# A dynamic convolution and squared-ReLU feed-forward kernel: the four-slot convolution from the sixth block on instead of the ninth

## The chip, the cores and the metric

The kernel runs on one core of one Trainium2 chip. The metric is the time of one execution in device microseconds (us). Five engines work side by side, each through its own list of instructions in order: PE (the matrix engine), DVE and ACT (vector and scalar engine), POOL and SP. In this kernel SP and POOL mainly issue transfers (DMAs); SP also issues the stores of the result. Tiles live in SBUF, a memory of 128 partitions; PE writes to PSUM, from which ACT and DVE copy.

## The reference, cut to what matters

```python
# dynamic convolution: x (8, 4096, 192), weight_gen (8, 4096, 8 heads, 7 taps)
w = softmax(weight_gen, over the 7 taps)
x_pad = six zero rows ahead of each sequence
out[b, s, h, g] = sum over k of w[b, s, h, k] * x_pad[b, s + k, 24 * h + g]
# feed-forward on the 32768 rows of out: 192 -> 2048 -> 192
h = maximum(out @ moe_w_in, 0)
return h * h @ moe_w_out
```

Each of the 8 heads owns 24 of the 192 columns and has its own seven weights at each position.

## The kernel before, in words

The 32768 positions are 64 sub-blocks of 512. They are worked in 33 blocks, counted from 0 here: the first two blocks hold one sub-block each, blocks 2 to 32 hold two. A block's work has four parts.

*Weights and bands.* ACT takes the exponential of the raw weights (line 238), DVE sums, inverts and multiplies (245, 252, 260) into `v_first` or `v_big`. For the first batch and the first half of the second these rows go by DMA from SBUF to the tiles `wr`, alternately on SP and POOL (`move_rows`, line 351); later they go through DRAM (`vd`). DVE multiplies `wr` with a mask into the band tiles `bd` (`st_bands`, line 391).

*The convolution, C.* PE multiplies the loaded `x` rows (`xt`, loaded on POOL, lines 311 to 321) with the bands into PSUM, and ACT or DVE copy the result as float16 to `y`, which has the channels on the partitions and 512 positions along the row, for two halves at once (partitions 0 to 63 and 64 to 127). There are two forms:

- The old form (`st_conv`, line 519) puts the 192 channels into three slots of 64. A tile of 32 partitions then holds parts of two heads, and each needs its own matmul with its own band: 120 matmuls of 8 to 32 columns for a block. ACT makes both copies (line 530).
- The four-slot form (`st_conv_spread`, line 485) gives each head a tile of 32 partitions with 24 used rows. Heads 0 to 5 take slots 0 to 2, heads 6 and 7 a fourth slot: 80 matmuls. ACT copies slots 2 and 3, DVE slots 0 and 1 (line 495). Then four DMAs on SP (line 499) move heads 6 and 7 in pieces of 8 rows from the fourth slot into the free rows of the other three, so that the matmuls that follow read three full slots in both forms.

Because the rows stand in another order, blocks with the four-slot form use `w_p`, a copy of `w_in` with its rows permuted in the same way. `load_w_spread` fills it with 16 DMAs from DRAM on POOL (lines 156 and 163), and `cross_w_spread` with two more that exchange the halves (line 169).

*The units, u.* Each block has 16 units (`st_unit`). PE makes 128 of the 2048 hidden channels from `y` and `w_i` or `w_p` (line 564) in a PSUM tile `h`, of which there are three, shared with C; ACT applies the ReLU (line 578), DVE squares it into `g` (line 582), two units at a time but for the last two.

*The second matmul, M.* Eight steps a block, two for each quarter of the positions, multiply the `g` of the block before with `w_o` (line 613). After the second of a quarter ACT copies one PSUM bank (line 627) and DVE adds the other (line 629); only then may the next quarter write there, as there is only one such pair of banks.

The order of all this is written out by hand, in strings of steps, and every engine keeps it. For blocks 0 to 3 the strings are spelled out in `plans`. From block 4 on two strings are used, and a table (`fill`) adds the softmax pieces (E, S), band steps (B) and weight loads (L) at certain units:

```python
steady = "MuMuuu" * 3 + "MuuuMCu"
steady_spread = "MuMuuu" * 2 + "MuCMuuu" + "MuMuuu"
```

A C in block j makes the convolution of block j + 1; it is followed by the x loads for block j + 2 on POOL. The four-slot form is used for blocks from `FIRST_SPREAD = 8` on, and the same name decides from which block on `steady_spread` is used and where the band steps stand. `load_w_spread` is issued after the C of block 5, `cross_w_spread` after that of block 6.

Of the kernel before, what the change touches and what calls it, by code (L numbers as in the profile page):

```python
# [9 lines left out]
def kernel(  # L10
# [34 lines left out]
    HK = H * KK  # L45
    G = D // H
    SPREAD = H - 2
    FIRST_SPREAD = 8
    HP = H // 2

    P = 128
# [87 lines left out]
    def cross_w_in(q):  # L139
        for r0, r1 in ((0, RT), (RT, 0)):  # L140
            nc.sync.dma_start(out=w_i[r0 : r0 + RT, q, 1], in_=w_i[r1 : r1 + RT, q, 0])
# [322 lines left out]
    def st_conv_spread(j):  # L464

        s0, n = BLOCKS[j]
        y = p_y.tile([P, NK + 1, TB], f16, name="y")
        y_t[j] = y
        for ks in ((NK, NK - 1), (0, 1)):
            yp = ps_h.tile([P, 2, TB], f32, name="yp", tag="h")  # L470
            k0 = min(ks)
            for k in ks:
                for i in range(NT):
                    a, b = bounds[i], bounds[i + 1]
                    for half in (0, 1):
                        s = s0 + half
                        hi = a + (STEP if tile_start(s, i) == starts[i] else b - a)
                        bd = bd_t[s][:, H * a : H * hi].rearrange(
                            "p (g c e) -> p g e c", g=HP, e=2
                        )  # L480
                        for e in (0, 1):
                            head = 2 * k + e
                            p0 = RT * half + 32 * e
                            c0 = min(G * head, D - 32)
                            nc.tensor.matmul(  # L485
                                out=yp[p0 : p0 + 32, k - k0, a:b],
                                lhsT=x_t[s][:, i, c0 : c0 + 32],
                                rhs=bd[:, head // 2, e, 0 : b - a],
                                start=True,
                                stop=True,  # L490
                                skip_group_check=True,
                                tile_position=(0, p0),
                            )
            copy = nc.vector.tensor_copy if k0 == 0 else nc.scalar.copy
            copy(out=y[:, k0 : k0 + 2], in_=yp)  # L495
        for p0 in range(0, P, 32):
            head = SPREAD + p0 // 32 % 2
            r0 = p0 + G * head - min(G * head, D - 32)
            nc.sync.dma_start(out=y[p0 + G : p0 + 32, 0:NK], in_=y[r0 : r0 + G, NK])

    def st_conv(j):

        if j >= FIRST_SPREAD:
            return st_conv_spread(j)
        if j < NFIRST:
            return st_conv_first(j)
        y = p_y.tile([P, NK, TB], f16, name="y")
        y_t[j] = y
        yps = [ps_h.tile([P, 2 * TB], f32, name="yp", tag="h") for _ in range(2)]
        for later, s, i, q, half, a, b, base in conv_pieces(j):  # L510
            lo = bounds[i]
            hi = lo + (STEP if tile_start(s, i) == starts[i] else bounds[i + 1] - lo)
            _, ha, hb, pre = quads[q]
            m, h = (32, hb) if later else (pre, ha)
            bd = bd_t[s][:, H * lo : H * hi].rearrange("p (g c e) -> p g e c", g=HP, e=2)
            p0 = RT * half + 32 * (q % 2)
            k = q // 2
            col = TB * (k % 2) - base
            nc.tensor.matmul(  # L519
                out=yps[k // 2][p0 : p0 + m, col + a : col + b],  # L520
                lhsT=x_t[s][:, i, 32 * q : 32 * q + m],
                rhs=bd[:, h // 2, h % 2, a - lo : b - lo],
                start=True,
                stop=True,
                skip_group_check=True,
                tile_position=(0, p0),
            )
        for n, yp in enumerate(yps):
            k0, k1 = 2 * n, min(2 * n + 2, NK)
            nc.scalar.copy(  # L530
                out=y[:, k0:k1],
                in_=yp[:, 0 : (k1 - k0) * TB].rearrange("p (k c) -> p k c", c=TB),
            )
# [20 lines left out]
    def st_unit(j, u):  # L554

        w = w_p if j >= FIRST_SPREAD else w_i
        h = ps_h.tile([P, 2, TB], f32, name="h", tag="h")
        if j < NFIRST:
            first_unit(u, h, y_t[j])
        else:  # L560
            for slot in range(NK):
                for half, r0 in enumerate((0, RT)):
                    k = slot ^ half if slot < 2 else slot
                    nc.tensor.matmul(  # L564
                        out=h[:, half],
                        lhsT=w_in_chunk(w, u, slot, half),
                        rhs=y_t[j][r0 : r0 + RT, k],
                        start=(slot == 0), stop=(slot == NK - 1),
                        skip_group_check=True,
                        tile_position=(r0, 0),  # L570
                    )
        e = u % 2
        if e == 0:
            t1_t[j] = p_t1.tile([P, 2, 2, TB], f16, name="t1")
            gp_t[j] = p_g.tile([P, 2, 2, TB], f16, name="g")
        t1, g = t1_t[j], gp_t[j]
        g_t[(j, u)] = g[:, e]
        nc.scalar.activation(out=t1[:, e], in_=h, func=ActF.Relu)  # L578
        n = 2 if j < NFIRST or u < NF - 2 else 1
        if e + 1 >= n:  # L580
            a = e + 1 - n
            nc.vector.tensor_tensor(  # L582
                out=g[:, a : e + 1], in0=t1[:, a : e + 1], in1=t1[:, a : e + 1], op=AluOp.mult
            )
# [63 lines left out]
    with nc.allow_low_precision("fp16 matmul pipeline"), tc.manual_schedule():  # L648
# [71 lines left out]

        steady = "MuMuuu" * 3 + "MuuuMCu"
        steady_spread = "MuMuuu" * 2 + "MuCMuuu" + "MuMuuu"
        plans = {
            0: "B1 u u u u E1 C S1 u u M u u",
# [9 lines left out]
        def at(j, u, kind, *args):  # L736
            fill.setdefault((j, u), []).append((kind, *args))
# [36 lines left out]
        for j in range(len(plans), NBLK - 1):  # L774
            a = BLOCKS[j + 1][0]
            small = [p for p in parts if p.fb <= j + 1][-1].r == FIRST
            us = {4: (7, 9), 6: (7, 9)}.get(j, (5, 9) if small else (1, 5))
            if j + 1 >= FIRST_SPREAD:
                us = (1, 5)
            for n, u in enumerate(us):  # L780
                at(j, u, "B", a + n)
        for j in range(len(plans), NBLK):
            plan, u = [], 0
            for step in steady_spread if j + 1 >= FIRST_SPREAD else steady:
                if step == "u":
                    plan += [f"{kind}{n}" for kind, n in fill.get((j, u), ())]
                    u += 1
                plan.append(step)
            plans[j] = " ".join(plan)
# [3 lines left out]
        def load_rows(j):  # L793

            s = [p for p in parts if p.fb <= j][-1]
            if s.r == FIRST:
                return
            if s in stored:
                for n in range(BLOCKS[j][0], sum(BLOCKS[j])):
                    wr_load(n)  # L800
            else:
                waiting.append((s, j))
# [40 lines left out]
        for j in range(NBLK):  # L843
            if j + 2 < NBLK:
                load_rows(j + 2)
            if j == 1:
                for q in range(WQ):
                    cross_w_in(q)
            u = 0
            for step in plans[j].split():  # L850
                kind, n = step[0], int(step[1:] or 0)
                if kind == "u":
                    st_unit(j, u)
                    u += 1
                elif kind == "M":
                    next(mm2)
                elif kind == "C" and j + 1 < NBLK:
                    st_conv(j + 1)
                    if j == 0:
                        x_load(3)  # L860
                    elif j + 2 < NBLK:
                        for k in range(BLOCKS[j + 2][0], sum(BLOCKS[j + 2])):
                            x_load(k)
                    if j == 5:
                        load_w_spread()
                    elif j == 6:
                        cross_w_spread()
                elif kind == "E":
                    parts[n].exp(*next(parts[n].exps))
                elif kind == "S":  # L870
                    soft(parts[n])
                elif kind == "B":
                    st_bands(n)
                elif kind == "L":
                    parts[n].load(nc.sync)


        j = NBLK - 1
# [44 lines left out]
```

The softmax here doesn't subtract the row's maximum and nothing guards it: scores larger than these inputs give would overflow.

## Time and profile before

| | us |
|---|---|
| median of three runs | 733.32 (732.42 to 733.91) |
| the profiled execution | 733.26 |
| its span, first to last instruction | 731.5 |
| PE busy | 724.6 |
| DVE busy | 626.1 |
| ACT busy | 612.8 |
| POOL busy | 100.0 |

The profile is that of one execution. The span is shorter than the execution's time by what lies around the instructions. A busy time is the union of an engine's instructions. The chain that ended last gives each engine and line its share of the path that set the end. A timeline line shows the start within the span, the length, the engine, the line of the code, the operation and how many instructions were merged; in brackets stands the idle time before it and what ended it. The letters dq or q behind an engine name its queue: SPq lines are the issues of transfers, not the transfers.

Line numbers are those of the kernel before.

### The profile page before, as it was taken

How to read it: one execution, taken by the hardware profiler on the slowest of the kernel's cores; microseconds unless marked ns; L12 is line 12 of the kernel's file. 1: busy time of each engine (PE TensorE's matmuls, PEld its weight loads, DVE VectorE, ACT ScalarE, POOL GpSimd, SP SyncE). 2: the span in 40 equal slices, each digit the busy share in tenths (PEclk: the TensorE clock that was granted, in tenths of full speed). 3: DMA queues.
4: the chain of work that ended last, by engine and by line, in shares of the span. 5: the costliest groups of instructions: out<-in, count | busy, mean ns of one | idle time of the engine just before them, and what ended most of it. 6: DMA issues, size and time to landing. Idle time of an engine off the chain costs nothing.

```text
span 731.5 us, 30985 instructions
## 1 busy us (share of the span) xinstructions
PE 724.6 (99%) x14053; PEld 529.2 (72%) x14053; DVE 626.1 (86%) x834; ACT 612.8 (84%) x731; POOL 100.0 (14%) x145
## 2 busy tenths in 40 slices
PE   8999999999999999999999999999999999999998
PEld 4557788777777777777777777777777777777777
DVE  6898998998898988888988888988889988778753
ACT  5999888888888888888888888888888888888883
POOL 8232222321001100011000010010000110001000
PEclk9999999999999999999999999999999999999999
DMA  9555444784445452455433554334544315444012
GB/s 204 115 105 115 82 76 109 146 150 118 98 66 136 87 94 57 86 117 114 72 69 68 124 116 87 56 73 120 103 87 86 57 50 120 66 87 78 30 45 68
DMA packets 125984, 68.30 MB, mean 93 GB/s; under 512 B 85321, under 2 KB 122140, under 8 KB 125340
## 3 DMA queue, kind: packets, MB, share of 16 engines
q0 software_dynamic: 46192, 19.43, 22.5%
q1 hardware_dynamic: 79516, 46.79, 22.5%
q8 instruction: 110, 1.80, 1.0%
q14 instruction: 22, 0.18, 0.1%
q10 hardware_dynamic: 144, 0.10, 0.0%
HBM read 50.18 MB, written 28.70 MB: 108 GB/s over the span
## 4 chain that ended last, share of the span: by engine, by line
PE 92%; DVE 2%; issue 1%; DMA 0%; ACT 0%; DVEq 0%
PE o L613 45%; PE h L564 42%; PE yp L485 4%; PE yp L519 1%; DVE bd L391 1%; DVE g L582 1%; DMA wr<-v_first 0%; ACT t L578 0%; DVE v_first L260 0%; DVE rcp L252 0%; DVE ssum L245 0%; PE h L549 0%; DVE o_sb L629 0%; ACT o_sb L627 0%; DVEq L391 0%
## 5 line engine op out<-in xcount | busy, mean ns | idle before, releaser
L578 ACT ACTIVATE t<-h 128x1024 f16<-128x1024 f32 x512 | 496.6, 1026 | 60.3 <-PE h L564 58.9
L613 PEld LDWEIGHTS <-g 64*128 64x128 f16 (+1 forms) x8032 | 344.6, 94 | 54.9 <-issue 2.3
L613 PE MATMUL o<-w_o,g 64*128 64x192 f16 (+1 forms) x8032 | 380.4, 243 | 0.2 <-DVE o_sb L629 0.2
L582 DVE TENSOR_TENSOR g<-t 128x2048 f16<-128x2048 f16 (+1 forms) x287 | 307.4, 1105 | 28.3 <-ACT t L578 28.1
L564 PE MATMUL h<-y,w_p 64*128 64x512 f16 x2400 | 291.7, 376 | 0.0
L564 PEld LDWEIGHTS <-w_p 64*128 64x128 f16 x2400 | 113.9, 94 | 94.7
L391 DVE TENSOR_TENSOR bd<-wr,mask 128x4160 f16<-128x4160 f16 (+3 forms) x89 | 149.4, 1703 | 2.1 <-DMA wr<-v_first 1.2
L629 DVE TENSOR_TENSOR o_sb<-o,o_sb 128x384 f32<-128x384 f32 x123 | 68.4, 556 | 62.2 <-ACT o_sb L627 61.1
L321 POOL DMA_DIRECT2D xt<-in_x_dram x63 | 53.0, 844 | 415.2 <-PE yp L485 362.4
L627 ACT COPY o_sb<-o 128x384 f32<-128x384 f32 x129 | 61.7, 478 | 45.5 <-PE o L613 45.0
L564 PE MATMUL h<-y,w_i 64*128 64x512 f16 x576 | 70.8, 376 | 0.2 <-ACT y L530 0.2
L564 PEld LDWEIGHTS <-w_i 64*128 64x128 f16 x576 | 31.2, 94 | 21.4 <-issue 1.4
L485 PEld LDWEIGHTS <-xt 128*32 128x32 f16 x2000 | 24.4, 95 | 10.6 <-issue 10.6
L260 DVE TENSOR_TENSOR v_big<-ex,rcp 128x112 f16<-128x112 f32 (+5 forms) x180 | 29.9, 237 | 1.9 <-DMA vd<-v_big 0.9
L495 DVE CAST y<-yp 128x1024 f16<-128x1024 f32 x25 | 30.5, 1218 | 0.0
L485 PE MATMUL yp<-bd,xt 128*32 128x104 f16 (+1 forms) x2000 | 28.3, 210 | 0.0
L238 ACT ACTIVATE ex<-wg 128x560 f32<-128x560 f32 (+4 forms) x38 | 25.9, 683 | 2.0 <-DMA wg<-in_weight_gen_dram 2.0
L245 DVE TENSOR_REDUCE ssum<-ex 128x80 f32<-128x560 f32 (+4 forms) x38 | 25.3, 666 | 1.5 <-ACT ex L238 1.5
L495 ACT CAST y<-yp 128x1024 f16<-128x1024 f32 x25 | 25.2, 1006 | 0.0
L252 DVE RECIPROCAL rcp<-ssum 128x80 f32<-128x80 f32 (+4 forms) x38 | 22.8, 600 | 1.3
L311 POOL DMA_DIRECT2D xt<-in_x_dram x7 | 3.9, 555 | 123.8 <-PE yp L485 109.4
L351 POOL DMA_DIRECT2D wr<-v_first x24 | 12.9, 562 | 22.8 <-ACT t L578 12.2
(40 smaller groups left out, 117.2 us busy)
## 6 DMA issues: line engine op xcount, KB each, us to landing
out_dram<-o_sb SPq DMA_DIRECT2D x63, 384.0 KB
xt<-in_x_dram POOLq DMA_DIRECT2D x42, 240.0 KB, 4.8
wg<-in_weight_gen_dram SPq DMA_DIRECT2D x4, 1064.0 KB
xt<-in_x_dram POOLq DMA_DIRECT2D x21, 192.0 KB, 4.7
wr<-vd SPq DMA_DIRECT2D x38, 80.0 KB
vd<-v_big SPq DMA_DIRECT2D x5, 512.0 KB
y<-y SPq DMA_DIRECT2D x100, 24.0 KB
wg<-in_weight_gen_dram SPq DMA_DIRECT2D x3, 616.0 KB
```

The costliest lines, as they stand in the source:

```text
L238: nc.scalar.activation(out=self.ex[:, lo:hi].rearrange("p r g k e -> p (r g) k e"), in_=self.wg[:, lo:hi].rearrange("p r (g e) k -> p (r g ...
L260: eng.tensor_tensor(out=bass.AP(tensor=v.tensor, offset=v.offset + lo * H * SL + lo % SL * 2 + g * SL * 2, ap=[list(v.ap[0]), [H * SL + 2, ...
L321: eng.dma_start(out=dst[:, first:last], in_=ap)
L391: nc.vector.tensor_tensor(out=bd_t[j][:, H * lo : H * (lo + len(tiles) * n)].rearrange("p (g m c) -> p g m c", g=shape[1], c=2 * SL), in0= ...
L485: nc.tensor.matmul(out=yp[p0 : p0 + 32, k - k0, a:b], lhsT=x_t[s][:, i, c0 : c0 + 32], rhs=bd[:, head // 2, e, 0 : b - a], start=True, sto ...
L495: copy(out=y[:, k0 : k0 + 2], in_=yp)
L564: nc.tensor.matmul(out=h[:, half], lhsT=w_in_chunk(w, u, slot, half), rhs=y_t[j][r0 : r0 + RT, k], start=(slot == 0), stop=(slot == NK - 1 ...
L578: nc.scalar.activation(out=t1[:, e], in_=h, func=ActF.Relu)
L582: nc.vector.tensor_tensor(out=g[:, a : e + 1], in0=t1[:, a : e + 1], in1=t1[:, a : e + 1], op=AluOp.mult)
L613: nc.tensor.matmul(out=oo[:, cc * Dm : (cc + 1) * Dm], lhsT=g[r0 : r0 + n, cc * P : (cc + 1) * P], rhs=w_o[r0 : r0 + n, fc, :], start=(fc ...
L627: nc.scalar.copy(out=o_sb, in_=o[0][:, c])
L629: nc.vector.tensor_tensor(out=o_sb, in0=o[1][:, c], in1=o_sb, op=AluOp.add)
```

## The change

The four-slot form is used from block 5 on instead of block 8, so in three more blocks (5, 6 and 7). What else hung on the name `FIRST_SPREAD`, the choice of the string and the band steps, stays at 8 under a new name, `EARLY_CONV`. In `steady`, which orders blocks 4 to 6, C moves ahead of the last M. The 16 loads of `w_p` are issued after the C of block 1, behind the x loads there, and the two exchanges after the C of block 2.

```diff
-    FIRST_SPREAD = 8
+    FIRST_SPREAD = 5
+    EARLY_CONV = 8
...
-        steady = "MuMuuu" * 3 + "MuuuMCu"
+        steady = "MuMuuu" * 3 + "MuuuCMu"
...
-            if j + 1 >= FIRST_SPREAD:
+            if j + 1 >= EARLY_CONV:
                 us = (1, 5)
...
-            for step in steady_spread if j + 1 >= FIRST_SPREAD else steady:
+            for step in steady_spread if j + 1 >= EARLY_CONV else steady:
...
-                    if j == 5:
+                    if j == 1:
                         load_w_spread()
-                    elif j == 6:
+                    elif j == 2:
                         cross_w_spread()
```

## The prediction

> **What bounds the kernel now.** I read the page first (busy shares, the chain that ended last), then the PE timeline around two block boundaries, then ACT, DVE, SP and POOL over the same microseconds, and last the trace's DMA records.
>
> The page, its busy shares and the chain that ended last:
>
> ```profile
> span 731.5 us, 30985 instructions
> ...
> PE 724.6 (99%) x14053; PEld 529.2 (72%) x14053; DVE 626.1 (86%) x834; ACT 612.8 (84%) x731; POOL 100.0 (14%) x145
> ...
> PE o L613 45%; PE h L564 42%; PE yp L485 4%; PE yp L519 1%; DVE bd L391 1%; DVE g L582 1%; DMA wr<-v_first 0%; ACT t L578 0%; DVE v_first L260 0%; DVE rcp L252 0%; DVE ssum L245 0%; PE h L549 0%; DVE o_sb L629 0%; ACT o_sb L627 0%; DVEq L391 0%
> ```
>
> PE sets the end and is never idle for long: whatever PE is spared comes off the time, and whatever PE waits for is added. So I cost everything as PE time.
>
> PE's timeline where block 4 goes over into block 5 (columns: start, length, engine, line, operation):
>
> ```profile
> 95.43 1.48 PE L613 MATMUL o<-w_o,g 64*128 64x192 f16 x32
> 96.84 1.60 PE L519 MATMUL yp<-bd,xt 128*32 128x104 f16 x120
> 98.38 0.82 PE L564 MATMUL h<-y,w_i 64*128 64x512 f16 x6
> 99.03 1.66 PE L613 MATMUL o<-w_o,g 64*128 64x192 f16 x32
> 100.45 0.89 PE L564 MATMUL h<-y,w_i 64*128 64x512 f16 x6
> ```
>
> The order is M (a second-matmul step), C (120 matmuls), u15, M, and at 100.45 u0 of block 5, the first reader of the new y. From 95.43, which I call T, to u0 it is 5.02 us. At the next two boundaries T is 118.09 and 140.71 and u0 comes at 123.07 and 145.62 (4.98, 4.91).
>
> PE where block 7 makes the first four-slot conv:
>
> ```profile
> 156.07 0.81 PE L564 MATMUL h<-y,w_i 64*128 64x512 f16 x6
> 156.82 1.13 PE L485 MATMUL yp<-bd,xt 128*32 128x104 f16 x80
> 157.88 1.49 PE L613 MATMUL o<-w_o,g 64*128 64x192 f16 x32
> ```
>
> DVE and SP after that conv:
>
> ```profile
> 158.53 1.22 DVE L495 CAST y<-yp 128x1024 f16<-128x1024 f32 x1
> ```
>
> ```profile
> 159.82 3.01 SPq L499 DMA_DIRECT2D y<-y  x4
> ```
>
> The four-slot y isn't complete with the copies: four 24 KB moves on SP follow the DVE copy. In the DMA records I took, for each of the 25 such convs, when the last of the four landed after the DVE copy ended: 4.9 to 6.5 us, median 5.4, and 4.4 for the last one, which has no x loads beside it. Here they landed at 165.92; the first reader is at 167.70. Nobody waits, because seven units and three M lie between conv and reader.
>
> ACT and DVE at the end of block 4:
>
> ```profile
> 94.34 2.85 ACT L578 ACTIVATE t<-h 128x1024 f16<-128x1024 f32 x3
> ```
>
> ```profile
> 94.22 4.09 DVE L582 TENSOR_TENSOR g<-t 128x2048 f16<-128x2048 f16 x4
> 98.23 0.55 DVE L629 TENSOR_TENSOR o_sb<-o,o_sb 128x384 f32<-128x384 f32 x1
> ```
>
> The relu of the third unit ends at 97.19 (T+1.76), the square of it on DVE at 98.31 (T+2.88; T+2.78 and T+2.77 at the other two).
>
> [...] the undisturbed last case lands 4.4 us after the copy, of which the fourth issue begins 2.1 to 2.2 us in. [...] the wr loads issued on POOL at 59.11 landed 3.7 us later, just behind the x loads issued at 55.48 (6.3 to 6.9 us to landing). [...]
>
> **The change, part by part.**
>
> Conv matmuls: 3 blocks x (120 - 80). Old boundary: M at 95.43 and u15 at 98.38 are 2.95 apart, less 1.32 for a plain M is 1.63. New kind: 156.07 to 157.88 is 1.81, less 0.65 for the unit is 1.16. Saved 0.47 a block, 1.4 in all. The same from block periods: 22.54 between old convs (74.30, 96.84) against 22.08 between new ones (156.82, 178.90).
>
> Copies: ACT loses the 594 ns half copy of each block and DVE gains the 1.22 us one. The order of ACT's and DVE's instructions in the changed kernel puts both y copies ahead of the o copy and the o sum of the M that now follows C.
>
> The y moves, the main term. In blocks 4, 5 and 6 the order becomes u u u C M u15, and the next block opens with M, u0. Counting from T for block 4: conv 95.52 to about 96.7, M to 98.0, u15 to 98.65. The DVE copy is queued behind the squares, so it runs 98.31 to 99.53; the o sum behind it ends at 100.0. The opening M needs that bank, so it runs 100.0 to 101.4 instead of from 98.65. But u0 needs the four moves: 99.53 + 5.4 = 104.95 against 100.45 before, a loss of 4.5. The other two: 120.87 + 1.22 + 5.4 = 127.5 against 123.07 (4.4) and 143.48 + 1.22 + 5.4 = 150.1 against 145.62 (4.5). Sum +13.4; these are u0-to-u0 differences, so the 1.4 saved and the wait of the opening M are inside. The squares can't come earlier, since ACT's relu of the third unit bounds them. Bounds: landing 4.9 gives 11.9, landing 6.2 gives 15.8. On SP only an output store stands behind the moves, with nobody waiting for it. Behind the waiting u0 stands all of PE; ACT and DVE catch up meanwhile, so nothing later is late, but a bound PE doesn't win the time back.
>
> The loads of w_p. They leave POOL's queue at 123 and 148, where nobody waited (gain nothing), and enter at 43.3, behind the x loads of conv 2. POOL before:
>
> ```profile
> 42.43 0.84 POOL L321 DMA_DIRECT2D xt<-in_x_dram  x1
> ...
> 59.11 2.72 POOL L351 DMA_DIRECT2D wr<-v_first  x5 [2.87 <-DVE v_first L260]
> ```
>
> The 16 loads took 12.3 us at 123.23 to 135.56, with 3.1 of waiting for landings eight DMAs back; so from 43.3 to about 55.5. The x loads of block 4 (before: 54.08) go to about 55.6 to 57.8. The two crossing moves wait until the loads have landed (median 5.7 us), about 60.3, and hold POOL till then; behind them stand the wr loads of sub-blocks 6 and 7, and then the x loads issued after conv 4, not due before 96.84. So the wr loads are issued at 61.7 instead of 59.11. In the ring they stand behind 768 KB of crossing, which took 6.6 and 7.5 us to land: near 68.5, wr near 69. Their reader on DVE:
>
> ```profile
> 64.40 0.56 DVE L629 TENSOR_TENSOR o_sb<-o,o_sb 128x384 f32<-128x384 f32 x1 [1.19 <-ACT o_sb L627]
> 64.87 2.32 DVE L391 TENSOR_TENSOR bd<-wr,mask 128x4160 f16<-128x4160 f16 x1
> ...
> 69.63 0.56 DVE L629 TENSOR_TENSOR o_sb<-o,o_sb 128x384 f32<-128x384 f32 x1 [0.17 <-ACT o_sb L627]
> ```
>
> The band starts at 64.87 with the wr landed some 2 us before. If it starts at 69, two squares and the o sum behind it end at 69 + 5.1 = 74.1, and the M that needs that bank, on PE at 70.86, waits 3.3. Bounds: landing at 66.5 costs 0.8, at 71.5 costs 5.8; no gain is possible.
>
> Sum: 733.26 (the profiled execution, 0.06 under the median) + 13.4 + 3.3 = 749.96, so 750.0.
>
> **Rivals.** *The band isn't late.* If POOL's loads land faster than at 123, or the crossing doesn't hold the wr loads back in the ring, only the y moves count: 733.3 + 13.4 = 746.7. [...] Against: the crossing alone needs 6.6 us. *The stalls grow.* Before u0 PE has nothing from 101.4 to 104.95, 3.5 us, [...] The full clock in every slice of before speaks for nothing either way, as no such gap occurs. *Faster:* one mechanism, at the opening units of blocks 5, 6 and 7: if the moves land within 0.9 us of the copy's end (T+4.1 against the old u0 at T+5.0), the M between C and u15 and the opening M cover them, and if the w_p loads are covered too 1.4 remains as gain: 731.9. Against: all 25 measured landings are over 4.3.
>
> **How the numbers follow.** Main case (both stalls) 0.66, own range 746.5 to 754; band not late 0.2; growing stalls 0.12; faster or hidden 0.02. What a measurement of this kernel tells from no change is about 0.2%, 1.5 us; 731.9 lies on that edge, so its chance is split: faster 0.01, same 0.01, slower 0.98. Range 744.5 to 755.5: the low end is 11.9 with the band nearly in time, the high end adds the longer landings or the clock.
>
> **What would show it.** Right: PE idle before the first unit of blocks 5, 6, 7 by about 3.5 us, released by a y move, and before the opening M by DVE's o sum; one PE gap near 71 behind a DVE wait on wr; conv groups 3 x 120 and 28 x 80. Wrong: no idle before u0 (landings hidden), a band on time, or a granted clock below 1 behind the gaps.

## The result and the profile after

The changed kernel takes 758.16 us (median of four runs, 754.96 to 759.53) against 733.58 for the kernel before; the ratio is 1.0332, 95% interval 1.0297 to 1.0366. That is slower, as forecast, but 8 us more than the 750.0 predicted and above the range's upper end of 755.5. The profiled execution took 758.13.

The page of the changed kernel, its busy shares and the chain that ended last:

```profile
span 756.4 us, 30766 instructions
...
PE 736.1 (97%) x13933; PEld 533.5 (71%) x13933; DVE 629.8 (83%) x837; ACT 612.2 (81%) x728; POOL 99.1 (13%) x145
...
PE 86%; DMA 4%; DVE 2%; POOL 1%; issue 1%; ACT 1%; SPq 0%; DVEq 0%; POOLq 0%
```

PE has 120 matmuls fewer, yet its busy time grew by 11.5 us. The waits alone can't do that: with fewer matmuls, busy time grows only if matmuls take longer. DMA, at 0% in the chain before, holds 4% of it.

The list of waits shows which waits are new or have grown on PE and DVE (the time in total, how often, the longest; PEld is PE's loading of weights). In the kernel before, PE waited for no y move and only 0.2 us for the o sum, and DVE 1.2 us for `wr`:

```profile
PEld L565 <- DMA y<-y: 11.0, 6, 3.5
PE h L565 <- DMA y<-y: 9.4, 4, 3.3
PE o L614 <- DVE o_sb L630: 5.0, 5, 2.8
DVE bd L392 <- DMA wr<-v_first: 4.8, 2, 3.9
```

PE's timeline from block 4 to block 5, where the predicted order C, M, u15, M, u0 is to be seen:

```profile
99.47 1.46 PE L486 MATMUL yp<-bd,xt 128*32 128x104 f16 x80
100.86 1.49 PE L614 MATMUL o<-w_o,g 64*128 64x192 f16 x32
102.19 0.81 PE L565 MATMUL h<-y,w_i 64*128 64x512 f16 x6
102.92 0.24 PE L614 MATMUL o<-w_o,g 64*128 64x192 f16 x1
103.92 1.48 PE L614 MATMUL o<-w_o,g 64*128 64x192 f16 x31 [0.76 <-DVE o_sb L630]
107.73 1.55 PE L565 MATMUL h<-y,w_p 64*128 64x512 f16 x6 [2.34 <-DMA y<-y]
108.66 2.86 PE L614 MATMUL o<-w_o,g 64*128 64x192 f16 x30
```

The opening M waits for the o sum, u0 waits for the moves, both as written down. The last line is the surprise: 30 matmuls of M in 2.86 us, where 32 took 1.49 at 100.86.

DVE in the same place, and earlier at the late band; below it POOL with the exchange and the wr loads:

```profile
68.09 2.33 DVE L392 TENSOR_TENSOR bd<-wr,mask 128x4160 f16<-128x4160 f16 x1 [3.86 <-DMA wr<-v_first]
...
102.18 1.22 DVE L496 CAST y<-yp 128x1024 f16<-128x1024 f32 x1
103.31 0.55 DVE L630 TENSOR_TENSOR o_sb<-o,o_sb 128x384 f32<-128x384 f32 x1
```

```profile
59.99 1.28 POOL L170 DMA_DIRECT2D w_p<-w_p  x2 [2.85 <-issue]
61.24 2.73 POOL L352 DMA_DIRECT2D wr<-v_first  x5
```

PE at the M that the late band holds up:

```profile
70.14 0.24 PE L614 MATMUL o<-w_o,g 64*128 64x192 f16 x1
73.21 1.66 PE L614 MATMUL o<-w_o,g 64*128 64x192 f16 x31 [2.83 <-DVE o_sb L630]
74.55 1.60 PE L565 MATMUL h<-y,w_i 64*128 64x512 f16 x6
75.83 2.49 PE L614 MATMUL o<-w_o,g 64*128 64x192 f16 x32
```

Again the matmuls after the gap are slow, until about 78. The table by stretches, cut where the granted clock changes (columns: stretch, its length, busy time and instructions of PE, weight loads, DVE, ACT, POOL, then PE's granted clock, 1.00 being full speed, the DMA share and GB/s), shows why:

```profile
71.00:74.40 3.40, 1.19 (x30) 1.19 (x31) 3.40 (x4) 2.34 (x3) 0.00 (x0) 0.99 0.00 0
74.40:77.80 3.40, 3.40 (x38) 2.92 (x34) 3.40 (x5) 1.02 (x1) 0.00 (x0) 0.50 0.02 5
105.00:108.50 3.50, 1.14 (x14) 0.47 (x11) 3.02 (x11) 0.00 (x0) 0.11 (x1) 1.00 0.88 177
108.50:111.90 3.40, 3.40 (x40) 3.09 (x36) 0.00 (x0) 1.19 (x2) 2.60 (x5) 0.50 0.35 62
132.40:135.80 3.40, 0.87 (x21) 0.64 (x16) 1.55 (x6) 0.62 (x1) 0.00 (x0) 1.00 1.00 137
135.80:142.60 6.80, 6.05 (x49) 4.11 (x51) 1.19 (x3) 1.81 (x3) 0.00 (x0) 0.50 0.64 158
163.10:166.50 3.40, 0.55 (x5) 0.09 (x1) 2.79 (x11) 0.00 (x0) 0.00 (x0) 1.00 1.29 182
166.50:173.30 6.80, 5.90 (x48) 3.99 (x50) 1.48 (x2) 2.06 (x3) 0.00 (x0) 0.50 0.41 111
```

Each of the four gaps is followed by a stretch at half clock. M took about twice its time there (2.86 against some 1.5), so about half of PE's busy time in these stretches is lost: half of 3.40 + 3.40 + 6.05 + 5.90 = 18.75 us, an estimated 9.4. So the 24.9 us between the two spans come apart:

| term | predicted | measured | how measured |
|---|---|---|---|
| waits around u0 of blocks 5, 6, 7, conv gain inside | 13.4 | 12.5 | from the end of the three units to u0: 8.35, 9.11 and 10.04 us against 5.02, 4.98 and 4.91 |
| the M behind the late band | 3.3 | 2.8 | PE's idle time at 73.21 |
| half clock | 0 | 9.4 | PE busy in the half-clock stretches, halved |
| sum | 16.7 | 24.7 | spans: 24.9 |

(The third u0 is taken from 167.40, where its last five matmuls run after two waits of 2.82 and 0.94; the 0.1 us of the matmul that ran between them is taken off the sum. In this execution PE reaches the M behind the band at 70.14, 0.7 us earlier than in the one before, so the sum can be held against the spans to about that.)

### The profile page after: what moved, and what is told of

Read it like the earlier page. It is cut to its first block, busy times and chain, and to the rows that moved or that the text cites. A ratio compares the mean times of both kernels' runs of the same rounds, so it can differ in the third digit from the quotient of the medians.

```text
span 756.4 us, 30766 instructions
## 1 busy us (share of the span) xinstructions
PE 736.1 (97%) x13933; PEld 533.5 (71%) x13933; DVE 629.8 (83%) x837; ACT 612.2 (81%) x728; POOL 99.1 (13%) x145
## 4 chain that ended last, share of the span: by engine, by line
PE 86%; DMA 4%; DVE 2%; POOL 1%; issue 1%; ACT 1%; SPq 0%; DVEq 0%; POOLq 0%
PE o L614 43%; PE h L565 39%; PE yp L486 4%; DMA y<-y 2%; DMA wr<-v_first 1%; ACT t L579 1%; DMA xt<-in_x_dram 1%; DVE g L583 1%; DVE bd L392 1%; PE yp L520 0%; POOL wr L352 0%; POOL w_p L157 0%; SPq L500 0%; POOL w_p L164 0%; DMA w_p<-in_moe_w_in_dram 0%
## 5 line engine op out<-in xcount | busy, mean ns | idle before, releaser
L614 PE MATMUL o<-w_o,g 64*128 64x192 f16 (+1 forms) x8032 | 389.5, 245 | 5.0 <-DVE o_sb L630 5.0
L614 PEld LDWEIGHTS <-g 64*128 64x128 f16 (+1 forms) x8032 | 351.9, 95 | 59.8 <-issue 9.4
L565 PE MATMUL h<-y,w_p 64*128 64x512 f16 x2688 | 335.6, 379 | 9.4 <-DMA y<-y 9.4
L565 PEld LDWEIGHTS <-w_p 64*128 64x128 f16 x2688 | 131.9, 95 | 118.8 <-DMA y<-y 11.0
L486 PEld LDWEIGHTS <-xt 128*32 128x32 f16 x2240 | 27.6, 95 | 12.7 <-issue 12.7
L565 PE MATMUL h<-y,w_i 64*128 64x512 f16 x288 | 35.9, 382 | 0.1
L496 DVE CAST y<-yp 128x1024 f16<-128x1024 f32 x28 | 34.1, 1218 | 0.0
L486 PE MATMUL yp<-bd,xt 128*32 128x104 f16 (+1 forms) x2240 | 32.3, 209 | 0.4
L496 ACT CAST y<-yp 128x1024 f16<-128x1024 f32 x28 | 28.2, 1009 | 0.0
L565 PEld LDWEIGHTS <-w_i 64*128 64x128 f16 x288 | 15.1, 95 | 12.2 <-issue 1.6
L352 POOL DMA_DIRECT2D wr<-v_first x24 | 13.0, 564 | 22.3 <-ACT t L579 11.9
```

Source lines behind the costliest of these rows:

```text
L486: nc.tensor.matmul(out=yp[p0 : p0 + 32, k - k0, a:b], lhsT=x_t[s][:, i, c0 : c0 + 32], rhs=bd[:, head // 2, e, 0 : b - a], start=True, sto ...
L565: nc.tensor.matmul(out=h[:, half], lhsT=w_in_chunk(w, u, slot, half), rhs=y_t[j][r0 : r0 + RT, k], start=(slot == 0), stop=(slot == NK - 1 ...
L614: nc.tensor.matmul(out=oo[:, cc * Dm : (cc + 1) * Dm], lhsT=g[r0 : r0 + n, cc * P : (cc + 1) * P], rhs=w_o[r0 : r0 + n, fc, :], start=(fc ...
```

## The experiments

**The early w_p loads alone.** The kernel before, with only the two conditions moved:

```diff
-                    if j == 5:
+                    if j == 1:
                         load_w_spread()
-                    elif j == 6:
+                    elif j == 2:
                         cross_w_spread()
```

> The kernel before with one part of the change alone: the 16 loads of w_p and the two exchanges issued after the C of blocks 1 and 2; convolution forms and order as before. Theory (the wr loads stand behind the exchange in POOL's ring, DVE's band is late, one M waits, and the clock is halved for one stretch after that gap): 2.8 us of wait plus half of a 3.41 us stretch, 1.7, so 4.5 over before, about 738.1. Rival (the loads are covered and the y moves make the whole loss): 733.6, no PE gap near 70 us.

Measured: 737.92 us, ratio 1.0067 (1.0052 to 1.0082). The M behind the band, on PE's timeline of this kernel:

```profile
74.02 2.71 PE L613 MATMUL o<-w_o,g 64*128 64x192 f16 x31 [3.88 <-DVE o_sb L629]
```

The gap is 3.88, the M behind it takes 2.71 us where 1.48 is usual, and the mean granted clock of the profile is 0.998. The rival, that the loads are covered, falls: these 18 transfers cost 4.8 us though no matmul waits for their data. The total fits the theory better than its parts, as the gap was put at 2.8. The trace of the changed kernel shows two delays for the `wr` loads on POOL: they were issued 2.1 us later (61.24 against 59.11) and landed 4.9 to 6.0 us after their issue, against 2.7 to 3.7 before. No run shows what each would cost alone, nor that the place behind the exchange is what made the landing slow.

**No moves.** The changed kernel, without the four y moves in blocks 5 to 7. Heads 6 and 7 then never reach the three slots that the matmuls read there, so this kernel leaves out two of the eight heads in these blocks and stands for its time alone:

```diff
-        for p0 in range(0, P, 32):
+        for p0 in range(0, P, 32) if j >= EARLY_CONV else ():
```

> The changed kernel without the four y moves on SP in blocks 5, 6 and 7 (this leaves out 8 of the 24 rows of each head's slot there). Theory (u0 waits for the moves): the waits on moves and the half clock behind them are gone; what stays is the late band with its clock stretch (4.5) and the opening M's wait for DVE's o sum, about 1.0 a block: 733.6 + 4.5 + 3.0 = 741, full clock from 80 us on. Rival (the loss comes from C standing ahead of M, that is from the o sum behind the y copy, and the moves are hidden): about 755.

Measured: 740.91, ratio 1.0108 (1.0093 to 1.0123). The waits on PE's timeline are the band's and the three of the opening M:

```profile
75.26 2.72 PE L614 MATMUL o<-w_o,g 64*128 64x192 f16 x31 [4.53 <-DVE o_sb L630]
...
105.71 1.48 PE L614 MATMUL o<-w_o,g 64*128 64x192 f16 x31 [0.74 <-DVE o_sb L630]
...
129.02 1.48 PE L614 MATMUL o<-w_o,g 64*128 64x192 f16 x31 [0.57 <-DVE o_sb L630]
...
152.39 1.48 PE L614 MATMUL o<-w_o,g 64*128 64x192 f16 x31 [0.64 <-DVE o_sb L630]
```

The granted clock is 0.93 from 55 to 80 us, with the M at 75.26 in 2.72, and 1.00 from 80 to 180; the rival (about 755) falls. The moves, with the clock they cost, are worth 758.2 - 740.9 = 17.3 us, some 70% of the loss. It is a rough figure, since the band's gap is 4.53 here and 2.83 in the changed kernel's profile.

**Filler.** Are the half-clock stretches a cause or just a mark of idle time? PE was kept at work in the gap, with the waits left in place:

```diff
+            if u == 0 and FIRST_SPREAD <= j < EARLY_CONV:
+                for _ in range(10):
+                    nc.tensor.matmul(
+                        out=h[:, 0], lhsT=warm[:, 0:P], rhs=warm, start=True, stop=True,
+                        skip_group_check=True,
+                    )
             for slot in range(NK):
```

> The changed kernel with 10 extra matmuls (128x512, about 0.22 us each at full clock, 2.2 in all) into u0's own PSUM tile ahead of the first unit of blocks 5, 6 and 7, where PE waits for the y moves; the real matmuls overwrite them. Theory (the waits are 15 us, and the half clock behind them costs the rest): the waits stay and the stretches at half clock after 100 us (3.4 + 6.8 + 6.8 us) go, half of their sum, 8.5: about 749.7. Rival (the low clock is only a mark of idle time and costs nothing; the waits alone make 25 us): 758 or a little more.

Measured: 752.37, ratio 1.0266 (1.0249 to 1.0283): 30 matmuls more (ten take 2.33 us), 5.8 us less. PE at block 5:

```profile
105.42 2.33 PE L564 MATMUL h<-warm 128*128 128x512 f16 x10
108.03 1.20 PE L571 MATMUL h<-y,w_p 64*128 64x512 f16 x6 [0.28 <-DMA y<-y]
108.86 1.53 PE L620 MATMUL o<-w_o,g 64*128 64x192 f16 x30
```

u0 starts 8.46 after the start of its conv at 99.57 (8.26 without filler), so the wait is the same, but M takes 1.53 and not 2.86, and the granted clock is 1.00 from 105.2 to 112.0. The clock is the cause of that part. The run fell 2.7 short of what I expected. One half-clock stretch stayed behind two waits of 0.76 and 0.97 close together: M takes 2.86 there, at 163.88, and the granted clock from 160 to 180 is 0.91, which makes an estimated 3.6 us at half; that explains 1.8. Another 0.8 is in the expectation itself, which halved whole stretches, though PE was idle for 0.75 and 0.90 us of two of them.

**Hidden w_p loads.** The conditions after C are taken out, and the loads follow the softmax step that issues block 4's wr loads, the exchange that of block 5's:

```diff
                     soft(parts[n])
+                    if (j, u, n) == (3, 0, 3):
+                        load_w_spread()
+                    elif (j, u, n) == (4, 0, 4):
+                        cross_w_spread()
```

> The changed kernel with the 16 loads of w_p issued behind the wr loads of block 4 (softmax step S3 in block 3) and the exchange behind the wr loads of block 5 (S4 in block 4). Theory: the late band and its clock stretch are gone, 758.2 - 2.8 - 1.7 = 753.7. Rival (the loads take other transfers' place wherever they stand): 758, with a wait elsewhere.

Measured: 750.81, ratio 1.0245 (1.023 to 1.0261). The gap near 71 is gone, and 7.4 us are won, not 4.5. The clock explains a good half of the rest: its mean of 0.991 over 749.0 us makes an estimated 13.5 us at half instead of 20.5. The stretch behind the band is gone, and the one at block 6 is shorter: the 17 matmuls of units behind its slow M take 2.10 us at 134.96, against 3.02 at 140.78 in the changed kernel.

**Both cures.** Hidden loads and 12 filler matmuls:

> The changed kernel with both cures: w_p loads behind the wr loads, and 12 extra matmuls (about 2.6 us) ahead of the first unit of blocks 5, 6 and 7. Theory (waits and half clock add): with the late band (2.8) and all half-clock stretches (9.4 us of work lost) gone, 758.2 - 12.2 = 746, with no stretch or at most one short one at half clock; what stays over the kernel before is the waits on the moves, about 12.5. Rival (the two cures act on the same time): 750 or more.

Measured: 746.12, ratio 1.0176 (1.0159 to 1.0193). The mean granted clock is 1.000, and no M from 55 to 185 us takes more than 1.54. What stays over the kernel before is 13.0 us; the trace put the waits around u0 at 12.5. The filler fills these waits and hardly changes their length: from the start of conv to u0 it is 8.55, 8.36 and 10.08 us, against 8.26, 9.02 and 9.95 in the changed kernel. So the terms of the table add up, and the rival, that the cures act on the same time, falls.

**C put back behind M.**

```diff
-        steady = "MuMuuu" * 3 + "MuuuCMu"
+        steady = "MuMuuu" * 3 + "MuuuMCu"
```

> The changed kernel with C put back behind the last M. Theory (u0 waits for the chain copy, issue, landing that starts at C): C starts 1.3 us later, the opening M doesn't wait for the o sum; u0 comes about 0.7 later a block, the gap grows to about 5 us [...]: 762, between 759 and 766. Rival (the place of C ahead of M makes the loss): below 755.

Measured: 762.47, ratio 1.0408 (1.038 to 1.0436); the runs spread from 760.1 to 766.3. The band's wait and two of the three waits of u0 on PE's timeline:

```profile
72.99 1.48 PE L614 MATMUL o<-w_o,g 64*128 64x192 f16 x31 [2.66 <-DVE o_sb L630]
...
108.05 2.03 PE L565 MATMUL h<-y,w_p 64*128 64x512 f16 x6 [5.64 <-DMA y<-y]
...
139.03 1.99 PE L565 MATMUL h<-y,w_p 64*128 64x512 f16 x6 [5.83 <-DMA y<-y]
```

Starting the chain of copy, issue and landing later makes the gap longer (5.64 and 5.83 us against 2.34 and 3.28). From the end of the three units, u0 comes 2.2, 1.4 and 0.7 us later than in the changed kernel, not 0.7 each. Moving C ahead of M is a help within this change, not its fault. The first line matters too: after a gap of 2.66 us M takes 1.48 here, its time at full clock, where a half-clock stretch followed 2.83 us in the changed kernel.

**The order alone.** The kernel before with "MuuuCMu" in place of "MuuuMCu":

> The kernel before with only C moved ahead of the last M in blocks 4 to 6; old form, w_p loads as before. Theory: the opening M of blocks 5, 6 and 7 waits for DVE's o sum, which has only u15 (0.65 us) to hide behind; 0.5 to 1.0 a block, no half clock, 733.3 + 2.3 = 735.6. Rival (the order is free, the waits on the o sum in the changed kernel come from DVE's y copy alone): 733.3.

Measured: 735.82, ratio 1.004 (1.0026 to 1.0053). PE's timeline shows the opening M waiting in all three blocks, and one M more in block 6:

```profile
98.88 1.48 PE L613 MATMUL o<-w_o,g 64*128 64x192 f16 x31 [0.35 <-DVE o_sb L629]
122.08 1.48 PE L613 MATMUL o<-w_o,g 64*128 64x192 f16 x31 [0.35 <-DVE o_sb L629]
134.00 1.48 PE L613 MATMUL o<-w_o,g 64*128 64x192 f16 x31 [1.28 <-DVE o_sb L629]
146.73 1.48 PE L613 MATMUL o<-w_o,g 64*128 64x192 f16 x31 [0.35 <-DVE o_sb L629]
```

These are 2.3 us, the size expected, but in part by luck: the three opening M wait 0.35 each, less than the 0.5 to 1.0 expected, and 1.28 lies at a place that I hadn't named. There DVE had just waited 2.7 us for the buffer of a store (`vd`), 0.86 in the kernel before; that this comes of the order isn't shown. The old conv between M and u15 was the cover of the o sum.

**C early.** The moves under real cover, in all three blocks, with the w_p loads as in the run that hid them:

```diff
-        steady = "MuMuuu" * 3 + "MuuuCMu"
+        steady = "MuMuuu" * 2 + "MuMuCuu" + "MuMuuu"
+        steady_6 = "MuMuuu" * 2 + "MuMuuuC" + "MuMuuu"
...
-            us = {4: (7, 9), 6: (7, 9)}.get(j, (5, 9) if small else (1, 5))
+            us = {4: (5, 7), 5: (5, 7), 6: (7, 8)}.get(j, (5, 9) if small else (1, 5))
```

> Four-slot form in blocks 5, 6 and 7 with the moves under cover: C after ten units in blocks 4 and 5 (six units and three M ahead of the reader) and after twelve in block 6, bands two to four units earlier, w_p loads behind the wr loads as in the run that hid them. Theory: no wait over 1 us and no half clock, the 1.4 us of matmuls is won less about 1 at the third boundary: 733, between 731.5 and 735. Rival (the four-slot form itself costs in these blocks, through DVE, which has softmax work there): 738 or more.

Measured: 740.56, ratio 1.0104 (1.009 to 1.0117). The mean granted clock is 1.000, and only the third u0 waits for moves. But other waits have come up:

```profile
91.75 1.39 PE L486 MATMUL yp<-bd,xt 128*32 128x104 f16 x78 [0.88 <-DVE bd L392]
...
104.45 0.34 PE L614 MATMUL o<-w_o,g 64*128 64x192 f16 x4 [1.15 <-DVE g L583]
...
143.06 1.11 PE L486 MATMUL yp<-bd,xt 128*32 128x104 f16 x78 [1.30 <-DVE bd L392]
...
151.97 0.37 PE L565 MATMUL h<-y,w_p 64*128 64x512 f16 x1 [1.14 <-DMA y<-y]
```

C now waits for the second band, and an M waits for the square of the last unit, which stands behind the softmax pieces on DVE. My theory got the moves right and the time wrong: as the bands are placed here, DVE has no room for them that early; other places weren't tried. The nine waits that the timeline names, four of them shown, sum to 6.5 us; against a loss of 7.6 in time and a matmul gain put at 1.4, over 2 us were not followed up.

**C early, two blocks.** As before, with block 7 in the old form and block 6 in its old order:

> As the run with C early, but block 7 keeps the old form and block 6 its old order, so only blocks 5 and 6 change form. Theory: 0.47 a block is won and nothing waits: 733.1 - 0.9 = 732.2, which is not to be told from no change. Rival (DVE): 736 or more.

Measured: 737.0, ratio 1.0056 (1.0042 to 1.007). The same waits as above at blocks 5 and 6, none at block 7, and a mean granted clock of 1.000. The rival's side again. No version tried beats the kernel before; by the prediction's count of matmuls, the most that could be won is 1.4 us.

## Why the prediction was wrong in size, point by point

- *PE sets the end, so waits on PE are added one for one:* right, with 24.7 of the 24.9 us found.
- *120 matmuls fewer, 1.4 us:* the counts are as predicted, the gain isn't. In its new place, behind three units, C takes 1.39 us from its start to that of the next step (99.47 to 100.86), against 1.54 in the old form (96.84 to 98.38): about 0.15 a block, not 0.47. The timeline with both cures shows what holds it up, a wait in the middle of C for ACT's relu, which frees one of the three `h` tiles:

```profile
95.92 0.65 PE L486 MATMUL yp<-bd,xt 128*32 128x104 f16 x40 [0.16 <-ACT t L585]
```

  The u0-to-u0 figures hold this already, so the sum didn't suffer.
- *The y moves, 13.4:* right in mechanism and nearly in size, 12.5. The landings came 4.7, 5.6 and 6.1 us after the DVE copy by the DMA records, where I had put 5.4. Without the moves the waits at u0 vanish. The sum rests on measured landings alone. (99.53 + 5.4 is 104.93, not 104.95; the loss of 4.5 stands.)
- *The w_p loads and the late band, 3.3:* right in each of its times. The exchange went out at 59.99 (predicted 60.3) and landed 6.0 to 6.4 us after its issue, the wr loads went out at 61.24 (61.7), the band started at 68.09 (69), PE's wait was 2.8. With the transfers of `w_p` issued behind the wr loads, the wait is gone. That the exchange holds back the landing of the wr loads behind it was my estimate; no run shows it by itself.
- *The rival of growing stalls, chance 0.12:* this is the step that failed. The half clock was left out of the sum 733.26 + 13.4 + 3.3, put at nothing there, and kept as an unlikely extra, whose size was my estimate and shown by no trace; no working is given for its small chance. It came at all four gaps of the profiled execution, an estimated 9.4 us. The rival named the waits before u0 alone, of 3.5 us, and left out the gap behind the band. The gaps before the half clock were of 2.3 to 3.3 us, in stretches where PE was still busy for 16 to 35%, and two of the four half-clock stretches lasted 3.41 us, the other two 6.83.
- *The range:* its upper end, 755.5, lay 5.5 us over the sum, which left room for some loss of clock or for longer landings, but not for 9.4. Adding 9.4 to the predicted sum gives 759.4, with the measured 758.2 just below. The lower end, 744.5, lies 0.7 below the sum that it names, 733.3 + 11.9.

## What to carry to other kernels

A wait that opens on a PE that is otherwise never idle can cost more than its length: here the work behind such waits ran at a granted clock of 0.50, an estimated 9.4 us on top of the 15.3 of the waits. So read the granted clock behind a wait, not the wait alone. Transfers that nobody reads soon weren't free here, with small urgent ones behind them in the same queue: the 18 of `w_p` cost 4.8 us by themselves, and issuing them behind the urgent ones won 7.4. When a step is made to end in a transfer, count the wait for the copy, the copy, issue and landing (here 7 to 8.5 us from the end of the conv) against the work ordered between it and its reader, and check that the work which then covers it isn't cover for something else.

## What was unexpected of the hardware

- In the changed kernel's trace the granted clock is 0.50 in four stretches, from 74.36, 108.50, 135.80 and 166.52 us, each behind waits of PE. In the 3.4 or 3.5 us ahead of them PE was idle for 2.21, 2.36, 2.53 and 2.85 us. How much idle time it takes, these runs don't show: with filler, half clock followed two waits of 0.76 and 0.97 us; with C behind M, the gap of 2.66 us that ends at 72.99 was followed by full clock. The stretches lasted 3.41 us where PE was busy throughout (from 74.36 and 108.50), and 6.83 where PE was still idle at the start (for 0.75 and 0.90 us); whether that decides the length wasn't tested.
- The runs with half clock spread more: the changed kernel's lie 4.6 us apart and those with C behind M 6.2, against 1.5 for the kernel before, at a granted clock of 1.000, and 0.5 for the kernel with both cures, at 0.999 to 1.000. The changed kernel's shortest run (754.96 us) has a mean granted clock of 0.989, the other three 0.986; with C behind M the shortest (760.10) has 0.986, the longest (766.34) 0.982. What makes the clock differ between runs of one kernel wasn't tested. The band's gap, too, changes between runs whose code up to there is the same: 2.66, 2.83, 2.84, 3.88 and 4.53 us in five profiles.
